# A window of four on the swapped weight loads of a recurrent attention kernel

## The chip, the cores and the metric

The kernel runs on one core of one Trainium2 chip. A core has a matrix engine (PE, with its weight loads shown apart as PEld), a vector engine (DVE), a scalar engine (ACT), a general engine (POOL) and an engine that only issues DMAs and waits (SP). Sixteen DMA engines move data between the chip's memory (HBM) and the core's on-chip memory. The metric is device time in microseconds (us) of one launch: before the change three runs gave a median of 1762.69 us (1759.73 to 1764.29).

## The reference, cut to what matters

Two branches are computed from `A_x`, 2048 rows of 640, and mixed by a gate. Branch b is a gated feed-forward layer without recurrence. Branch a is an attention over 64 segments of 32 rows: each segment attends over its rows and 8 memory rows, and the first 8 output rows of a segment are the memory of the next one.

```python
mem = mem0                                     # 8 rows of 640
for s in range(64):
    h = concat([mem, x[32*s:32*s+32]])         # 40 x 640
    q, k, v = (einsum('td,dhe->hte', h, W) for W in (Wq, Wk, Wv))   # 32 heads of 192
    p = softmax(where(mask, q @ k.T * scale, -1e9))
    o = einsum('hte,hed->td', p @ v, Wo)       # 40 x 640
    mem = o[:8]
    outs.append(o[8:])
a = concat(outs)
b = (gelu(x @ w_gate) * (x @ w_up)) @ w_down
out = g * a + (1 - g) * b                      # g = sigmoid((x * gate_w).sum(-1))
```

The segments can't be computed at the same time: the memory rows make a chain. Each of the four attention weights has 640 x 6144 numbers of two bytes, 31 MB in all, and each segment uses all of them. The on-chip memory holds most of them but not all.

## The kernel before, in words

**Two stages.** First the feed-forward branch runs for all rows (`ffn_*`, in the trace up to about 195 us); its result goes to a scratch tensor in HBM. Then come the 64 segments, `segment(s)`, of some 24 us each.

**Weights in pieces.** `Wq`, `Wk` and `Wv` are cut into pieces `(m, octet, k)`: matrix 0, 1 or 2, one of four groups of eight heads, and one of five slices of the 640 inputs. Such a piece is 128 partitions of 3072 bytes, 384 KB. `Wo` is cut into 16 pieces `(3, p)` of 128 partitions of 3840 bytes, 480 KB. Nearly all pieces have a place of their own in the big on-chip tensor `arena` and stay there. Sixteen places are shared by two pieces each (`partner`, lines 545 to 552): 13 of the first three matrices (five of V, five of K, three of Q), between octet 0 and octet 3, and three of `Wo`, between the first three and the last three pairs.

**Swapping.** Even segments go through the octets upwards, odd ones downwards (`octet`, line 527). So what a segment uses last, the next one uses first. A segment begins with the pieces that are there; after their last use in this segment `swap_loads` (line 612) loads the partner into the same place, and the partner is used at the segment's end. This makes 16 swapped loads in each of the segments, issued by `load_piece` (line 597; the DMA is line 599). Each place has its own semaphore (`slot0`, `slot1`, ...), which counts 16 when a load has landed; the PE instruction that first uses the piece waits for it.

**Order.** `PROG` (line 506) is an order written out by hand: projections `("g", group, k)`, transposes, scores, softmax, and output projections `("wo", ...)`, among which other work is placed. `_Sched.add` (line 73) records each operation in this order and derives what it has to wait for from the regions that it reads and writes; `finalize` turns these into semaphore waits and leaves out a wait that an earlier one on the same engine has covered (`wm`, `snap`). Each engine then runs its own list in order. In the segments SP issues all DMAs but two, so SP's list holds, in the order of `PROG`: the swapped loads of K and Q, the loads of V, the store of the last segment's output (`out_store`, line 956), the load of the next segment's rows (`x_load`, line 706), the last V piece, stores of prepared rows for later segments (`left_evac`, line 1276, and `left_store`, line 895), three `Wo` pieces, and loads of prepared rows and of branch b (`stg_load`, line 935; `bz_load`, line 947; `bzl_load`, line 952). A swapped load waits for the PE work that read the old piece. SP does nothing else while it waits, and what stands behind in its list isn't issued.

**The lines of PE** that are named below: 1046 and 226 are the projections, 884 those of prepared rows, 1087 to 1100 the scores, 1144 and 1149 the transposes of the softmax, 1177 and 1179 the products with v, 1206 and 1229 the output projection. Line 1375 is the DVE transpose that hands the memory rows to the next segment.

Of the kernel before, what the change touches and what calls it, by code (L numbers as in the profile page):

```python
# [231 lines left out]
def _build(nc, A_x, A_mem0, A_Wq, A_Wk, A_Wv, A_Wo, seg_len, w_gate, w_up, w_down,  # L232
# [34 lines left out]
    S_ = _Sched(nc)  # L267
# [82 lines left out]
    def bview(o, nbytes, plo=0, phi=128):  # L350
        return arena[plo:phi, o // 2:(o + nbytes) // 2]
# [4 lines left out]
    def sreg(o, nbytes, plo=0, phi=128):  # L356
        return Rg("sb", o, o + nbytes, plo, phi)
# [133 lines left out]
    def piece_src(key):  # L491
        if key[0] == 3:
            return Wo2[:, key[1]]
        m, o_, k = key
        return (Wq2, Wk2, Wv2)[m][:, k, OW * o_:OW * (o_ + 1)]

    def piece_size(key):
        return GO if key[0] == 3 else GQ

    def piece_view(key, o):  # L500
        if key[0] == 3:
            return bview(o, GO).rearrange("p (c n) -> p c n", n=Dm)
        return bview(o, GQ)
# [59 lines left out]
    res_off = {}  # L563
# [8 lines left out]
    r_res = {key: sreg(o, piece_size(key)) for key, o in res_off.items()}  # L572
# [13 lines left out]
    slot_id = {}  # L586
# [6 lines left out]
    later = []  # L593

    loaded = {}

    def load_piece(key, name):
        loaded[slot_id[key]] = key
        S_.add("sp", lambda e: e.dma_start(piece_view(key, res_off[key]), piece_src(key)), writes=[r_res[key]],
               dma_sem="slot%d" % slot_id[key], name="%s %s" % (name, key))  # L600

    def piece(seg, key):
        order = orders[seg % 2]
# [8 lines left out]
    def swap_loads(seg, item):  # L612
        if item[0] == "g" and item[1] == 0 and 0 < item[2] < KT - 1:
            later.extend(key for key in done_keys if key[0] == 1)
            done_keys[:] = [key for key in done_keys if key[0] != 1]
        elif later:
            done_keys[:] = sorted(done_keys + later, key=lambda key: key[:1] + key[2:])
            del later[:]
        for key in done_keys:
            other = swap_in.get(key)  # L620
            if other is None or (other in partner) == (seg % 2 == 0):
                continue
            load_piece(other, "swap s%d" % seg)
        del done_keys[:]
# [11 lines left out]
    def load_residents(cls, pick=lambda key: True):  # L636
        for key in first:
            if slot_class[key] == cls and pick(key):
                load_piece(partner[key] if key in tmp_off else key, "res")
# [39 lines left out]
    for h in range(NH):  # L679
        for w_, sb_, rw_, nm in ((w_gate, wg_sb, r_wg, "wg"), (w_up, wu_sb, r_wu, "wu")):  # L680
            S_.add("sp", lambda e, h=h, w_=w_, sb_=sb_: e.dma_start(
                sb_[h], w_.rearrange("(p k) f -> p k f", p=128)[:, :, FH * h:FH * (h + 1)]),
                writes=[rw_[h]], dma_sem="%s%d" % (nm, h))
# [228 lines left out]
    for n, (g, o) in enumerate(units):  # L912
# [7 lines left out]
        if g == 0:  # L920
            S_.add("pool", lambda e, o=o, b=b: e.tensor_copy(out=stg[o // 2][:, o % 2], in_=lst[b][:, 0]), reads=[r_lst[b]], writes=[r_stgh[o // 2][o % 2]],
                   name="stg s0 o%d" % o)
# [498 lines left out]
def bass_gated_mix__memory_aug_recurrent_mem_tr__glu_gated_geglu__prompt_kernel(  # L1421
    nc,
    A_x,
    A_mem0,
    A_Wq,
    A_Wk,
    A_Wv,
    A_Wo,
    A_seg_len,
    B_x,  # L1430
    B_w_gate,
    B_w_up,
    B_w_down,
    gate_w,
    out,
):
    _build(nc, A_x, A_mem0, A_Wq, A_Wk, A_Wv, A_Wo, A_seg_len, B_w_gate, B_w_up, B_w_down, gate_w, out)
# [33 lines left out]
```

## Time and profile before

| what | value |
|---|---|
| median of three runs | 1762.69 us (1759.73 to 1764.29) |
| span of the profiled execution, which is also its own time | 1765.1 us |
| PE busy | 1623.9 us, 92% |
| DVE, ACT, POOL busy | 960.0, 802.8, 320.0 us |
| granted PE clock, mean | 0.994 |
| moved by DMA | 499.57 MB, mean 283 GB/s |
| time of the DMA engines taken by SP's and ACT's DMAs (q1 and q10) | 78.3% and 0.6% |
| chain that ended last, by engine | PE 71%, DVE 15%, DMA 6%, issue 4%, ACT 4% |
| median from issue to landing, pieces of Wq, Wk, Wv, Wo | 5.4, 7.1, 9.1, 6.4 us |

The profile shows one execution. A group of instructions is named by its line, engine, output and inputs; "idle before" is the time the engine waited before these instructions, with what ended the wait. "Issue" there means that no semaphore explains the wait. SP's instructions are only the issues of DMAs; when a transfer has landed is told by the last update of its semaphore. The trace also holds a record of each DMA packet with its queue, start, duration and size, and of all semaphore updates. The span's first 195 us are the feed-forward stage; 1550 of the 1765 us are segments.

### The profile page before, as it was taken

Reading aid. Unit: us, or ns where it says so; the run is one execution under the profiler, and the core shown is the slowest. Engines: PE = TensorE matmul, PEld = TensorE weight load, DVE = VectorE, ACT = ScalarE, POOL = GpSimd, SP = SyncE. Lnnn points to the kernel's source line nnn. Section 1 sums busy time; section 2 is a strip of 40 time slices with the busy share of each in tenths; the row PEclk is TensorE's granted clock in tenths of the full one; section 3 lists DMA queues with packets and bytes.
Section 4 is the critical chain, followed back from the end, with each engine's and each line's share of the span. In section 5 each row is a group of like instructions: output and inputs, shape, how many; then the busy total and the mean of one; then the engine's idle time right before and its main releaser. Section 6 shows DMA issues by size and latency. Waiting matters only on the chain.

```text
span 1765.1 us, 80301 instructions
## 1 busy us (share of the span) xinstructions
PE 1623.9 (92%) x39162; PEld 809.5 (46%) x31501; DVE 960.0 (54%) x2932; ACT 802.8 (45%) x1835; POOL 320.0 (18%) x1099
## 2 busy tenths in 40 slices
PE   9999999999999999999999989999999998999887
PEld 4554444444444444454444444454444444454444
DVE  2222655556555655555555655555555655655554
ACT  3222544545444544444444544444444544445443
POOL 1100111111112112111212111111211121121211
PEclk9999999999999999999999999999999999999999
DMA  9814987888778887888788887879787886879776
GB/s 335 295 48 157 329 313 250 320 313 288 280 269 311 299 308 253 315 290 319 281 280 293 296 293 250 314 285 323 279 280 275 311 310 241 312 282 327 283 275 238
DMA packets 271311, 499.57 MB, mean 283 GB/s; under 512 B 105304, under 2 KB 132208, under 8 KB 270960
## 3 DMA queue, kind: packets, MB, share of 16 engines
q1 hardware_dynamic: 267832, 491.34, 78.3%
q8 instruction: 276, 4.52, 1.0%
q10 hardware_dynamic: 3128, 3.09, 0.6%
q14 instruction: 75, 0.61, 0.1%
HBM read 473.22 MB, written 21.11 MB: 280 GB/s over the span
## 4 chain that ended last, share of the span: by engine, by line
PE 71%; DVE 15%; DMA 6%; issue 4%; ACT 4%; DVEq 0%; SPq 0%; ACTq 0%
PE ps L1046 20%; PE ps L226 15%; PE ps L1206 8%; DMA arena<-in_A_Wo_dram 5%; PE ps L1177 3%; PE ps L804 3%; PE ps L801 3%; PE ps L884 3%; PE ps L1100 3%; PE ps L819 2%; PE ps L1087 2%; DVE ps L1114 2%; DVE arena L1112 2%; PE ps L1095 2%; PE ps L1229 2%
## 5 line engine op out<-in xcount | busy, mean ns | idle before, releaser
L1046 PE MATMUL ps<-arena 128*32 128x384 bf16 x9940 | 723.0, 329 | 42.4 <-DVE arena L1375 34.4
L226 PE MATMUL ps<-arena 128*32 128x384 bf16 x7680 | 595.4, 328 | 7.9 <-DVE arena L1215 3.5
L1046 PEld LDWEIGHTS ps<-arena 128*32 128x32 bf16 x9940 | 257.5, 97 | 365.3 <-issue 226.0
L1080 DVE STREAM_TRANSPOSE arena<-arena 128x384 bf16<-128x384 bf16 x512 | 270.8, 557 | 150.8 <-ACT arena L1066 149.2
L1066 ACT ACTIVATE arena<-ps 128x384 bf16<-128x384 f32 x512 | 236.2, 489 | 211.6 <-PE ps L1046 196.3
L1206 PE MATMUL ps<-arena 128*32 128x320 bf16 x6144 | 293.6, 301 | 13.9 <-issue 13.4
L1124 ACT ACTIVATE ps<-ps 104x160 f32<-104x160 f32 x256 | 71.9, 281 | 293.4 <-DVE ps L1114 293.4
L1206 PEld LDWEIGHTS ps<-arena 128*32 128x32 bf16 x6144 | 163.5, 97 | 74.0 <-issue 19.4
L1112 DVE TENSOR_REDUCE arena<-ps 104x4 f32<-104x160 f32 x256 | 83.0, 324 | 165.8 <-PE ps L1100 164.6
L941 POOL COPY arena<-arena 128x96 bf16<-128x96 bf16 x256 | 70.3, 275 | 513.4 <-PE ps L1100 444.2
L1188 ACT ACTIVATE arena<-ps 128x480 bf16<-128x480 f32 (+1 forms) x256 | 137.0, 535 | 43.8 <-PE ps L1179 39.6
L1196 POOL COPY arena<-arena 128x96 bf16<-128x96 bf16 x256 | 68.3, 267 | 441.1 <-ACT arena L1188 357.3
L1162 ACT ACTIVATE arena<-ps 128x448 bf16<-128x448 f32 x192 | 104.2, 543 | 96.7 <-PE ps L1149 96.4
L1069 ACT ACTIVATE arena<-ps 128x384 bf16<-128x384 f32 x256 | 125.1, 489 | 20.9 <-PE ps L1046 16.3
L1177 PE MATMUL ps<-arena 128*64 128x160 bf16 x1536 | 123.1, 243 | 12.5 <-ACT arena L1162 6.9
L1126 DVE TENSOR_REDUCE arena<-ps 104x4 f32<-104x160 f32 x256 | 83.0, 324 | 92.5 <-ACT ps L1124 92.5
L1177 PEld LDWEIGHTS ps<-arena 128*64 128x64 bf16 x1536 | 80.8, 109 | 91.6 <-issue 31.7
L884 PE MATMUL ps<-arena 128*32 128x384 bf16 x1280 | 111.4, 330 | 2.2 <-issue 2.0
L1179 PE MATMUL ps<-arena 128*64 128x64 bf16 x1536 | 104.8, 193 | 4.1 <-issue 4.1
L891 DVE STREAM_TRANSPOSE arena<-arena 128x384 bf16<-128x384 bf16 x128 | 73.7, 576 | 31.6 <-ACT arena L889 27.8
L1215 DVE TENSOR_TENSOR arena<-ps,arena 64x160 f32<-64x160 f32 x160 | 50.8, 317 | 72.3 <-ACT arena L1212 61.6
L1114 DVE TENSOR_TENSOR ps<-ps,arena 104x160 f32<-104x160 f32 x256 | 85.0, 332 | 8.8
(84 smaller groups left out, 1819.2 us busy)
## 6 DMA issues: line engine op xcount, KB each, us to landing
arena<-in_A_Wk_dram SPq DMA_DIRECT2D x335, 384.0 KB, 7.1
arena<-in_A_Wv_dram SPq DMA_DIRECT2D x335, 384.0 KB, 9.1
arena<-in_A_Wo_dram SPq DMA_DIRECT2D x205, 480.0 KB, 6.4
arena<-in_A_Wq_dram SPq DMA_DIRECT2D x209, 384.0 KB, 5.4
arena<-left_qk_scratch SPq DMA_DIRECT2D x126, 96.0 KB, 2.8
left_qk_scratch<-arena SPq DMA_DIRECT2D x49, 192.0 KB, 2.3
left_qk_scratch<-arena SPq DMA_DIRECT2D x30, 96.0 KB, 5.7
ffn_b_scratch<-arena ACTq DMA_DIRECT2D x16, 160.0 KB, 4.4
```

The costliest lines, as they stand in the source:

```text
L226: return e.add_instruction(mybir.InstMatmult(name=nm, start_tensor_calc=like["start"], stop_tensor_calc=stop, tile_size=(128, 32), tile_po ...
L884: fns.append(lambda e, outp=outp, rhs=rhs, j=j: e.matmul(outp, lhs, rhs, start=(k == 0), stop=(k == KT - 1), tile_position=(0, 32 * j)))
L1046: fns.append(lambda e, outp=outp, rhs=rhs, j=j: e.matmul(outp, lhs, rhs, start=(k == 0), stop=(k == KT - 1), tile_position=(0, 32 * j)))
L1066: S_.add("act", lambda e, m=m, bk=bk: e.activation(out=rows_sb[m], in_=ps[:, bk, 0:384], func=ACTF.Copy), reads=[r_ps[bk]], writes=[r_rows ...
L1069: S_.add("act", lambda e, i=i, bk=bk: e.activation(out=v_sb[i % NVB].rearrange("p (c n) -> p c n", c=3), in_=ps[:, bk, 0:384].rearrange("p ...
L1080: S_.add("dve", lambda e: e.transpose(out=dst[:, :, 0:L], in_=rows_sb[m].rearrange("p (c r) -> p c r", r=L)), reads=[r_rows[m]], writes=[r ...
L1112: S_.add("dve", lambda e: e.tensor_reduce(out=mxs, in_=S3, axis=AX.X, op=ALU.max), reads=[rb], writes=[rst], name="smax max")
L1114: S_.add("dve", lambda e: e.tensor_tensor(out=S3, in0=S3, in1=mxb, op=ALU.subtract), reads=[rb, rst], writes=[rb], name="smax sub")
L1177: return [lambda e: e.matmul(full, v[:, e0:e0 + 64], PTm[:, i], start=True, stop=False, tile_position=(0, 64 * i), skip_group_check=True), ...
L1179: lambda e: e.matmul(part, vl[:, e0:e0 + 64], PTl[:, i], start=False, stop=True, tile_position=(0, 64 * i), skip_group_check=True)]
L1188: S_.add("act", lambda e: e.activation(out=apx(u[:, 0, 0, :], [[R, na], [3 * R, 4], [1, R]]), in_=ps[:, A, 0:na * W].rearrange("p (c t r) ...
L1206: fns.append(lambda e, i=i, t=t, j=j, gv=gv: e.matmul(ps[32 * j:32 * j + 32, bank, 0:2 * DJ].rearrange("p (h n) -> p h n", h=2), lhs2[i], ...
```

## The change

At most four swapped loads are under way. `load_piece` keeps a list of the swapped loads that were issued last; each further one gets, beside the waits that it had, a wait for the landing of the fourth last one. Loads whose name doesn't begin with "swap" (the first filling of the places) are not counted and get no wait. No operation is added to PE, ACT, DVE or POOL, and the order on every engine is the one of before.

```diff
     loaded = {}
+    NUW = 4
+    under_way = []
 
     def load_piece(key, name):
         loaded[slot_id[key]] = key
-        S_.add("sp", lambda e: e.dma_start(piece_view(key, res_off[key]), piece_src(key)), writes=[r_res[key]],
-               dma_sem="slot%d" % slot_id[key], name="%s %s" % (name, key))
+        op = S_.add("sp", lambda e: e.dma_start(piece_view(key, res_off[key]), piece_src(key)), writes=[r_res[key]],
+                    dma_sem="slot%d" % slot_id[key], name="%s %s" % (name, key))
+        if name.startswith("swap"):
+            under_way.append(op)
+            if len(under_way) > NUW:
+                op.deps.add(under_way.pop(0))
```

In the built program SP's list has 764 loads that wait for a landing of a place, where it had 7: twelve in each segment, since the first four of a segment wait for loads whose landing SP already knows from a wait on PE. Most of these loads also wait for PE; an instruction carries one wait, so 504 separate wait instructions are added to SP's 1795 instructions. The waits of PE are the same.

## The prediction

> **What bounds the kernel now.** I read the page first, then the waits of PE, the chain in one window, SP's own timeline, the DMA table, and last the packet records.
>
> ```profile
> span 1765.1 us, 80301 instructions
> PE 1623.9 (92%) x39162; PEld 809.5 (46%) x31501; DVE 960.0 (54%) x2932; ACT 802.8 (45%) x1835; POOL 320.0 (18%) x1099
> q1 hardware_dynamic: 267832, 491.34, 78.3%
> q8 instruction: 276, 4.52, 1.0%
> ```
>
> PE is the bound, with some 141 us idle. The last line matters here: a second queue brings instructions, 276 packets of 4.52 MB / 276 = 16,384 bytes. PE and PEld have 70,663 instructions, 256.0 per packet, so these packets are PE's instructions, 64 bytes each, one packet per 256.
>
> ```profile
> PE ps L1046 <- DVE arena L1375: 34.4, 48, 1.2
> PE ps L1144 <- DVE arena L1131: 25.0, 65, 0.7
> PE ps L1206 <- issue: 13.4, 14, 2.0
> ...
> PE ps L1229 <- DMA arena<-in_A_Wo_dram: 6.1, 10, 2.3
> ...
> PE ps L1046 <- issue: 5.4, 8, 1.3
> PE ps L1177 <- issue: 4.8, 6, 1.5
> PE ps L1179 <- issue: 4.1, 6, 1.3
> ```
>
> These are PE's waits (total us, times, longest). It waits for swapped weights only 6.6 us (6.1 and 0.5 for one Wk row), so the loads are nearly hidden. It waits 34 us in 48 gaps for nothing that a semaphore explains. Each of these 48 gaps ends 2.2 to 2.7 us after the start of a 16,384-byte packet: PE stood without instructions. The chain of waits between 564 and 569 us shows the third longest, whose packet started at 565.23:
>
> ```profile
> 565.32 0.51 PE ps L1206 x9
> 565.83 1.76 issue
> 567.59 0.72 PE ps L1206 x15
> ```
>
> Now SP in one segment (start, us, engine, line, operation, tiles, count):
>
> ```profile
> 600.65 2.17 SPq L599 DMA_DIRECT2D arena<-in_A_Wq_dram  x3
> 602.86 2.24 SPq L599 DMA_DIRECT2D arena<-in_A_Wk_dram  x4
> 605.15 2.58 SPq L599 DMA_DIRECT2D arena<-in_A_Wv_dram  x4
> 607.77 0.57 SPq L956 DMA_DIRECT2D out_dram<-arena  x1
> 608.38 0.47 SPq L706 DMA_DIRECT2D arena<-x_scratch  x1
> 608.90 0.43 SPq L599 DMA_DIRECT2D arena<-in_A_Wv_dram  x1
> ```
>
> An issue takes about 0.48 us, so twelve swaps are given out in 8 us, but they land 0.97 us apart (a DMA engine takes 0.121 us for a packet of 3072 bytes, and each has 8 of a piece). So up to nine are outstanding, and the DMA table shows it as time from issue to landing:
>
> ```profile
> arena<-in_A_Wk_dram SPq DMA_DIRECT2D x335, 384.0 KB, 7.1
> arena<-in_A_Wv_dram SPq DMA_DIRECT2D x335, 384.0 KB, 9.1
> ```
>
> **The added wait, on the loads.** Twelve loads of a segment are issued later. In the segment above, the last V load was issued at 608.90; it would now wait for the V load that landed at 614.39. It landed at 618.47, as its turn came. So the question is whether the engines ever run out of work. Four pieces are 4 x 0.97 = 3.88 us. The round trip is the time from a landing to the landing of a piece issued then on an empty queue. The first swap of a segment is the nearest row: its first packet starts 0.96 to 1.2 us after the issue's start, and it lands 3.3 us (least, queue empty) to 3.8 us (median of 63, other small transfers ahead) after. SP needs 0.1 us to go on after a wait (median 0.08 from release to the end of an issue that was waiting), 0.4 more where a separate wait instruction comes first. So the round trip is 3.4 to 3.9 us, under or at the 3.88. It is a cold start besides; in a running queue the slowest engine still has two pieces before it when the new one arrives. Carried through all segments in SP's order, a round trip of 3.6 us makes none of the 16 loads later by more than 0.12 us in the mean. I take 0; for the upper bound I take 4.2 us, between the median first swap and the slow ones (4.6 us): 0.3 us lost per round, three rounds, 0.9 us at a segment's end. Less than 0 is excluded as long as PE releases the places when it did: no load is issued earlier, and the order is kept.
>
> **What is queued behind on SP.** `out_store`, `x_load`, stores of prepared rows (L1276), `stg_load`, `bz_load` are issued 1 to 5 us later. They use the same queue behind the same loads: the `x_load` of 608.38 landed at 617.46, between two V loads. Waiting for them are POOL's copies, POOL is 18% busy, and they land when they did. The last swaps, of Wo, are issued about 1 us later, and after them SP is free again: 6 us idle in the segment shown. I take 0. The 504 more instructions on SP cost at most 504 x 0.06 us over 1550 us, beside the waiting.
>
> **The added wait, on instruction fetches.** The same DMA engines serve both queues. From the packet records and PE's instruction count I took for each fetch how far PE had got beyond the earliest point at which neighbouring fetches start. With no swap outstanding that is 0.95 us (median), with one to three 1.6 to 1.8, with four 2.8, with five to nine 3.0 to 3.7. So a fetch stands behind what has already been given to its engine, up to some 3.3 us. By the time to the last landing: over 4 us to go, 179 fetches with 46 stalls of 33.0 us; under 4 us, 83 fetches with one of 0.5 us.
>
> With the window the last landing is never more than about 3.9 us off (4.8 with Wo pieces of 1.2 us), and the newest piece reaches the engines only after 0.6 to 1.0 us, so 1.7 to 2.7 us of work stand before a fetch, where 3.3 or so stood. That cuts a fetch by 0.6 to 1.6 us. Cutting every gap by 0.5 us would take 20.5 of the 34 us, by 1.0 us 29.3. I take nearly all. Bounds: 0 (the row for four outstanding, little below the rows above it) and 34.
>
> **What is late next.** PE comes earlier, the loads don't. From each landing to the first PE instruction that waits for it, the smallest value of a segment is under 0.1 us in 21 of 64 segments and 1.5 us in the median. Where a gap goes, I count per segment only as much as this smallest value: 21.8 of the 34 us. It is cautious, since a stall ahead of the piece's release also moves the load.
>
> **Sum.** 1765.1 - 21.8 + 0 = 1743 us for the profiled execution, which lies 2.4 us above the median of the three runs; against the median I say **1742**, 1.2% faster. Its own range is 1729 (all 34 us) to 1757.
>
> **A rule against it.** The fetch's delay grows with the swaps outstanding, 0.95 to over 3 us, as above. The Trainium skill, DMA: Bandwidth & Descriptors, section Queues, rings and completion order, says that each DMA engine goes round the queues that have work, packet by packet; by that a fetch would wait no longer for nine pieces than for four, and the time would stay 1763. The trace speaks against it in the delays, at least for the first four pieces. The Trainium skill, Runtime: NRT & Kernel Launch, section Instruction fetch mechanics, calls the crossing of a block "mostly hidden"; by that there is nothing to gain either. 48 gaps of 34 us say that here it isn't wholly.
>
> **Rivals.** (A) No difference. An engine may take in a fixed amount, and four pieces may be enough to fill it: the delay flattens at five, and four are already at 2.8 of 3.3 us. Then gaps shrink by 0.3 us at most and what is won goes into waits for Wo: 1763, between 1758 and 1768. Against it: four outstanding in the rows of before are four wholly handed over; in the window the fourth is mostly still on its way.
>
> (B) Slower: the queue runs dry. Place: from the fifth swap of each segment. It decides from a round trip over 3.88 us. At 4.2 us the last loads are 0.9 us late; 21 segments have no room for that. Counted per segment as above, lateness of 0.2, 0.5 and 1.0 us gives -15.6, -4.6 and +18.7 us with the gaps gone, and +27 us with the gaps kept; it turns at 0.6 us. So 1.0 us gives 1781. For it: 5% of the issues take over 1.1 us instead of 0.43, and the median first swap takes 3.8. Against it: those are cold starts.
>
> **How the numbers follow.** The forecast has 0.62, A 0.18, B 0.20. The bound between a difference and none is 0.3%, 5.3 us, about what runs can tell (three runs spread over 4.6 us). The forecast is all faster, A the same, B slower. Range: the forecast's lower end with a little left out, 1732, up over A and into B as far as half its chance, 1771; some 0.1 is left out above, 0.05 below.
>
> **What would show it.** SP: waits in L601 on landings of Wk, Wq and Wv, hundreds of them; issue to landing of Wk and Wv falls from 7.1 and 9.1 to about 4. PE: "issue" falls from 34 to under 10 us. PE's waits for in_A_Wo_dram rise from 6.1 us, to 10 or 20. DMA bytes unchanged, and landings within a segment still 0.97 us apart: if they are 1.05 or more, B is right. If "issue" stays near 34 us, A is. The prediction would be wrong if a fetch is delayed by something that goes along with outstanding swaps but isn't caused by them, such as the DMA engines' rate itself, which stays.

## The result, and the profile after

The kernel became slower. The changed kernel takes 1834.15 us (median of four runs, 1829.96 to 1844.28); the kernel before took 1761.21 us beside it (four runs, 1754.96 to 1764.29). The ratio is 1.043, with an interval of 1.039 to 1.047. The forecast was 1742 us.

The profiled execution took 1829.96 us, with a span of 1828.2 us, 63.1 us more than the span of before. The lines behind the change stand six lower than before (the load itself is L601 instead of L599), so L1046, L1206 and L1229 are now L1052, L1212 and L1235. From the page of the changed kernel, its span, PE's busy time, the two DMA queues and the chain that ended last by engine:

```profile
span 1828.2 us, 80824 instructions
PE 1647.4 (90%) x39181; PEld 800.3 (44%) x31501; DVE 964.1 (53%) x2932; ACT 803.0 (44%) x1835; POOL 321.0 (18%) x1099
q1 hardware_dynamic: 267832, 491.34, 80.4%
q8 instruction: 276, 4.52, 1.0%
PE 59%; DMA 25%; DVE 11%; ACT 3%; issue 2%; SPq 0%; DVEq 0%; ACTq 0%
```

The packets and the bytes are those of before. In the chain, DMA went from 6% to 25% and "issue" (of any engine there) from 4% to 2%: the loads, which had hardly counted, now hold a quarter of it. PE's busy time also grew, by 23.5 us, though it does the same work. The waits of PE (total us, times, longest) say the same:

```profile
PE ps L1235 <- DMA arena<-in_A_Wo_dram: 52.0, 64, 3.0
PE ps L1052 <- DVE arena L1381: 31.3, 48, 0.7
PE ps L1150 <- DVE arena L1137: 27.9, 70, 0.7
PE ps L1052 <- DMA arena<-in_A_Wv_dram: 21.6, 31, 1.7
...
PE ps L1212 <- issue: 2.4, 3, 0.9
...
PE ps L1235 <- issue: 0.8, 2, 0.6
```

All "issue" waits together fell from 33.9 us in 48 gaps to 3.9 us in 7. All waits for DMA rose from 6.8 to 75.8 us: for `Wo` from 6.1 to 52.0, for V from nearly nothing to 21.6. The waits for DVE are where they were. So the 63.1 us are 23.5 of PE's busy time, 69.0 of waits for loads, 30.0 saved of "issue", and 0.6 of everything else.

The table of DMA issues (KB each, median us from issue to landing) answers the one of before:

```profile
arena<-in_A_Wk_dram SPq DMA_DIRECT2D x335, 384.0 KB, 4.9
arena<-in_A_Wv_dram SPq DMA_DIRECT2D x335, 384.0 KB, 4.7
```

They were 7.1 and 9.1 us. With four under way, 4.9 us from issue to landing means one landing each 4.9 / 4 = 1.225 us. Without the window the mean of a segment's first twelve landings had been one each 1.109 us. One segment on SP's timeline (start, us, engine, line, operation, tiles, count) shows how it goes:

```profile
646.49 1.72 SPq L601 DMA_DIRECT2D arena<-in_A_Wq_dram  x3
649.29 3.64 SPq L601 DMA_DIRECT2D arena<-in_A_Wk_dram  x4
653.61 3.52 SPq L601 DMA_DIRECT2D arena<-in_A_Wv_dram  x4
657.18 0.59 SPq L962 DMA_DIRECT2D out_dram<-arena  x1
657.82 0.46 SPq L712 DMA_DIRECT2D arena<-x_scratch  x1
659.23 0.33 SPq L601 DMA_DIRECT2D arena<-in_A_Wv_dram  x1
660.16 2.47 SPq L601 DMA_DIRECT2D arena<-in_A_Wo_dram  x3
```

Four K pieces that went out in 2.2 us now take 3.6, and the last V piece goes out 12.7 us after the first Q piece, where it was 8.3. Inside this run, a K piece issued at 650.25 us, right behind a Q landing at 650.23, landed at 654.51, 4.26 us later; the V piece issued at 653.61 landed at 659.16, 5.55 us later. Both are above the 3.88 us that the forecast took four pieces to last. SP's own waits show what held it:

```profile
SPq L601 <- DMA arena<-in_A_Wk_dram: 192.8, 197, 3.1
SPq L601 <- DMA arena<-in_A_Wq_dram: 139.0, 154, 2.7
```

Over 62 segments, the means of the landings relative to the segment's first swap issue are, in us (worked out from the semaphore updates; pieces 14 to 16 are those of `Wo`):

```
piece    1     4     8     12     16
before  3.93  7.70 12.04  16.13  21.35
after   3.73  7.47 12.43  17.21  23.47
```

For four pieces there is no loss, as nothing waits. From the fifth on it grows, to 2.1 us at the end of the segment. About half of that shows in the time of a segment, which rose from 24.65 to 25.65 us.

### The profile page after: what moved, and what is told of

It reads as the page before. It is cut to its first block, busy times and chain, and to the rows that moved or that the text cites. A ratio compares the mean times of both kernels' runs of the same rounds, so it can differ in the third digit from the quotient of the medians.

```text
span 1828.2 us, 80824 instructions
## 1 busy us (share of the span) xinstructions
PE 1647.4 (90%) x39181; PEld 800.3 (44%) x31501; DVE 964.1 (53%) x2932; ACT 803.0 (44%) x1835; POOL 321.0 (18%) x1099
## 4 chain that ended last, share of the span: by engine, by line
PE 59%; DMA 25%; DVE 11%; ACT 3%; issue 2%; SPq 0%; DVEq 0%; ACTq 0%
DMA arena<-in_A_Wo_dram 18%; PE ps L1052 17%; PE ps L226 14%; PE ps L1212 5%; DMA arena<-in_A_Wv_dram 3%; PE ps L810 3%; PE ps L807 3%; DMA arena<-in_A_Wk_dram 3%; PE ps L1106 2%; PE ps L825 2%; PE ps L1183 2%; PE ps L1093 2%; DVE ps L1120 2%; PE ps L890 2%; PE ps L1101 2%
## 5 line engine op out<-in xcount | busy, mean ns | idle before, releaser
L1052 PE MATMUL ps<-arena 128*32 128x384 bf16 x9940 | 734.9, 334 | 56.0 <-DVE arena L1381 31.3
L226 PE MATMUL ps<-arena 128*32 128x384 bf16 x7680 | 607.3, 335 | 8.9 <-DVE arena L1221 3.5
L1052 PEld LDWEIGHTS ps<-arena 128*32 128x32 bf16 x9940 | 259.4, 98 | 400.7 <-issue 227.1
L1086 DVE STREAM_TRANSPOSE arena<-arena 128x384 bf16<-128x384 bf16 x512 | 270.9, 558 | 157.3 <-ACT arena L1072 155.8
L1212 PE MATMUL ps<-arena 128*32 128x320 bf16 x6144 | 283.4, 299 | 2.4 <-issue 2.4
L1212 PEld LDWEIGHTS ps<-arena 128*32 128x32 bf16 x6144 | 158.1, 96 | 57.9 <-issue 3.7
L1235 PE MATMUL ps<-arena 128*32 128x160 bf16 x3072 | 82.2, 235 | 58.6 <-DMA arena<-in_A_Wo_dram 52.0
L890 PE MATMUL ps<-arena 128*32 128x384 bf16 x1280 | 108.2, 330 | 0.0
L1235 PEld LDWEIGHTS ps<-arena 128*32 128x32 bf16 x3072 | 53.3, 96 | 108.5 <-DMA arena<-in_A_Wo_dram 68.7
```

What stands on the lines that cost most here:

```text
L226: return e.add_instruction(mybir.InstMatmult(name=nm, start_tensor_calc=like["start"], stop_tensor_calc=stop, tile_size=(128, 32), tile_po ...
L890: fns.append(lambda e, outp=outp, rhs=rhs, j=j: e.matmul(outp, lhs, rhs, start=(k == 0), stop=(k == KT - 1), tile_position=(0, 32 * j)))
L1052: fns.append(lambda e, outp=outp, rhs=rhs, j=j: e.matmul(outp, lhs, rhs, start=(k == 0), stop=(k == KT - 1), tile_position=(0, 32 * j)))
L1086: S_.add("dve", lambda e: e.transpose(out=dst[:, :, 0:L], in_=rows_sb[m].rearrange("p (c r) -> p c r", r=L)), reads=[r_rows[m]], writes=[r ...
L1212: fns.append(lambda e, i=i, t=t, j=j, gv=gv: e.matmul(ps[32 * j:32 * j + 32, bank, 0:2 * DJ].rearrange("p (h n) -> p h n", h=2), lhs2[i], ...
L1235: S_.add("pe", [lambda e, j=j, c=c, g_=g_, p=p: e.matmul(ps[32 * j:32 * j + 32, OB2, SC:512], u[:, p % 4, c, 0:L], g_[:, c, DJ * j:DJ * (j ...
```

## The experiments

Three readings of this were to be told apart. **T**: the queue runs dry. The round trip of a piece in a running queue is about 4.9 us and four pieces don't fill it; with more pieces outstanding the loss goes. **S**: the loss comes from SP being held in the waits, with the other DMAs in its list behind it. **W**: the loss comes from the 504 added wait instructions themselves, whatever the number they wait for. A fourth, **V**, was added for the halves of pieces below: what counts is only the number of bytes under way, not the number or size of the pieces.

### The size of the window

The edit changes one number, to 3, 5, 6 or 8:

```diff
-    NUW = 4
+    NUW = 6
```

> Window of three instead of four. Theory T (the DMA engines run dry): with four, the trace of the changed kernel shows 4.85 us from issue to landing in the middle of a segment, 3.05 us until the first of the 16 engines has finished its share and 1.75 us more until the last has; that is 1.21 us per swap against 1.11 us before. With three the round trip stays at 4.6 to 4.85 us, 1.55 us per swap: thirteen swaps 0.44 us later each, 5.7 us at a segment's end, of which some 1.1 us is covered: 1760 + 62 x 4.6 = about 2045 us (1980 to 2110). Rival S (what stands behind the waiting SP is late, whatever the engines do): SP is held back by the landing of the third instead of the fourth last, 1.2 us more: 1834 + 62 x 1.2 = about 1910. Rival W (the 504 further wait instructions cost the time): as with four, 1834.

> Window of five. T: 5 x 1.11 = 5.5 us of work against a round trip of 4.85, the engines hardly run dry: landings 1.11 to 1.13 us apart as before, 1750 to 1775 us, PE's unexplained waits (issue) between the 4 us with four and the 34 us without a window. S: SP is still held in each segment from the sixth load on, about 1.1 us less than with four: 1834 - 25 = about 1810. W: 1834.

> Window of six. T: no engine runs dry for the window's sake: 1745 to 1765 us; if fetches are still shortened, issue on PE below 25 us and the time below 1755. S: SP is held less, half of the loss stays: about 1790. W: 1834.

> Window of eight, reached only late in a segment (before, up to nine were outstanding). T: as before the change, 1755 to 1765 us, issue on PE about 30 us. S: 1760 to 1775. W (the further wait instructions are all still there): 1834.

Measured, with the changed kernel (window 4) and the one before (no window) among them. Issue to landing is that of a piece behind a full window (in the row "none", of a piece with about eight others under way), split into the time to the first of the 16 engines' updates and the spread from there to the last; the waits of PE and the stretches at half clock (from the trace's clock records) are those of the profiled execution, in us:

```
window median   ratio (95%)               issue to landing    /N    DMA    issue half clock
3      1994.31  1.131 (1.126 to 1.136)    2.78 + 1.45 = 4.23  1.41  187.7   0    204.8
4      1834.15  1.043 (1.039 to 1.047)    3.20 + 1.70 = 4.90  1.23   75.8   3.9   67.4
5      1789.43  1.013 (1.008 to 1.017)    3.77 + 1.96 = 5.73  1.15   32.2  23.2   48.2
6      1760.72  0.9987 (0.9959 to 1.0015) 4.59 + 2.15 = 6.74  1.12   13.9  27.7   10.7
8      1769.81  1.0028 (1.0005 to 1.0052) 6.35 + 2.19 = 8.54  1.07    6.9  38.5    6.4
none   1762.54                            7.25 + 2.04 = 9.29   -      6.8  33.9   23.6
```

T's number for a window of three, 1980 to 2110 us, was met; S's 1910 and W's 1834 were not. It was met near its lower end, and T's reason only in part: T let the round trip stay at 4.6 to 4.85 us, and it fell to 4.23. In a window of three DMA has 38% of the chain that ended last. The page has a span and a busy time of PE of

```profile
span 1985.0 us, 80887 instructions
PE 1703.3 (86%) x39181; PEld 816.5 (41%) x31501; DVE 965.3 (49%) x2932; ACT 804.2 (41%) x1835; POOL 321.2 (16%) x1099
```

and PE waits for V and `Wo`, with no "issue" line left among its waits:

```profile
PE ps L1052 <- DMA arena<-in_A_Wv_dram: 104.7, 90, 3.4
PE ps L1235 <- DMA arena<-in_A_Wo_dram: 76.5, 78, 3.5
```

W is out by all four: windows of six and eight have wait instructions of the same kind, and stand at 0.9987 and 1.0028. The instructions are thus worth at most the 9 us of the latter interval's end. S expected 1790 us for a window of six and is out there, too: SP stands 323 us in waits for landings of swapped loads in that run (541 us with the window of four), and it costs nothing. For a window of five T expected 1750 to 1775 and S about 1810, and 1789 was measured, which is neither: the round trip of a fuller queue is longer still (5.73 us against 5 x 1.11 = 5.55 us of work), so five pieces are just short. For a window of eight T expected 1755 to 1765; 1769.8 is a little above, and within S's 1760 to 1775, so that run speaks for neither. In the window of five both kinds of waits of PE stand side by side:

```profile
PE ps L1235 <- DMA arena<-in_A_Wo_dram: 27.9, 34, 2.7
...
PE ps L1235 <- issue: 10.6, 13, 1.7
```

At six the first is nearly gone and the second is back:

```profile
PE ps L1235 <- DMA arena<-in_A_Wo_dram: 12.4, 17, 2.1
PE ps L1052 <- issue: 8.2, 14, 1.1
```

and at eight it is nearly all "issue":

```profile
PE ps L1212 <- issue: 12.3, 13, 1.6
PE ps L1052 <- issue: 9.3, 12, 1.2
```

So the two effects cross, and at no size tried did the loss through loads and the gain on fetches leave anything: the window of six, the best, can't be told from the kernel before. The column "/N", issue to landing over the window, is the time per landing when the window is full. It falls from 1.41 to about 1.07 to 1.12 us, which is the rate without a window; from there more pieces only wait longer at the engines. No version was faster than the kernel before by more than its interval.

### Halves by partitions

To keep the bytes of four pieces under way but wait in smaller steps, each swapped load was cut into two DMAs of 64 partitions, each with its own semaphore; the window then counts halves: eight (`half8`, the bytes of four pieces), ten, twelve, and none (`half_free`, the control).

```diff
-    NUW = 4
+    NUW = 8
...
+        for h in range(2):
+            op = S_.add("sp", lambda e, h=h: e.dma_start(piece_view(key, res_off[key])[64 * h:64 * h + 64], piece_src(key)[64 * h:64 * h + 64]),
+                        writes=[sreg(res_off[key], piece_size(key), 64 * h, 64 * h + 64)],
+                        dma_sem="slot%d%s" % (slot_id[key], "b" * h), name="%s %s" % (name, key))
```

> Each swapped piece is loaded by two DMAs, partitions 0 to 63 and 64 to 127, each with its own semaphore; at most eight such halves are under way, so as many bytes as with a window of four pieces, but counted in finer steps. Theory T (the engines run dry because a whole round trip, 3.05 us to the first engine's end and 1.75 us of spread between the engines, stands against the work in the window): a half has four packets less per engine, 4 x 0.121 = 0.48 us, so the round trip is 4.85 - 0.48 = 4.4 us against 8 x 0.555 = 4.4 us of work: the engines are just kept busy, 1765 to 1800 us. Rival V (the bytes in flight, or SP being held by landings, set the rate, whatever the step): as with four pieces, 1815 to 1850 us. Against both: 32 issues of 0.48 us are 15.4 us of a segment's 24.6 on SP; the run without a window tells what that costs.

> The same halves with no window: the control. Both theories: 1755 to 1775 us, PE's unexplained waits (issue) about 34 us as before. If SP's doubled issues cost something it shows here.

> Ten halves under way, the bytes of five pieces (which gave 1789 us). T: 10 x 0.555 = 5.55 us of work against 4.4 to 4.6 us: 1750 to 1768 us, issue on PE 15 to 25 us. V: 1780 to 1795 us.

> Twelve halves, the bytes of six pieces (1761 us). T: 1752 to 1765 us, issue on PE about 28 us. V: 1755 to 1768 us. Tells whether halves as such cost anything where the window doesn't.

The forecasts of all four runs, the control's too, lie between 1750 and 1850 us and were missed. All four take the same time: half8 2297.82 us (ratio 1.302, 1.295 to 1.308), half_free 2299.05 (1.304, 1.297 to 1.311), half10 2294.67 (1.299, 1.291 to 1.306), half12 2295.82 (1.299, 1.292 to 1.306). The cut itself costs 30%, with or without a window. From the page of the control, its DMA packets and one line of its issues:

```profile
DMA packets 287575, 499.70 MB, mean 217 GB/s; under 512 B 121560, under 2 KB 148464, under 8 KB 287216
```

```profile
arena<-in_A_Wv_dram SPq DMA_DIRECT2D x640, 192.0 KB, 6.5
```

The bytes are the same but they move at 217 GB/s instead of 283. In the packet records a packet of 3072 bytes takes 0.20 us (median) where it took 0.121, one of 3840 bytes 0.258 where it took 0.149, and an issue on SP, with the pause behind it, takes 0.64 us where it took 0.48. Why the packets are slower isn't shown. The loads have become the bound: a piece is 8 x 0.20 = 1.6 us of work for each engine, and PE waits 340 us for DMA. A half takes 6.23 us from issue to landing behind a full window of eight, and eight halves are 8 x 4 packets x 0.20 = 6.4 us of work, so this window covers its round trip; it hardly binds (SP waits 71 us for landings of swapped loads, against 541 us in the changed kernel) and costs nothing over its control (-1.2 us). These runs were meant to tell T from V and don't; they give the price of the cut, and one thing on the fetches, below.

### Halves by columns

The same with each piece cut along the row of every partition, so that a half still spans 128 partitions, with packets of 1536 bytes:

```diff
+    def half(x, h):
+        n = x.shape[1] // 2
+        return x[:, h * n:(h + 1) * n]
...
+        for h in range(2):
+            op = S_.add("sp", lambda e, h=h: e.dma_start(*(half(x, h) for x in (bview(res_off[key], piece_size(key)), piece_row(key)))),
+                        writes=[sreg(res_off[key] + h * (piece_size(key) // 2), piece_size(key) // 2)],
+                        dma_sem="slot%d%s" % (slot_id[key], "b" * h), name="%s %s" % (name, key))
```

> Control for finer steps: each swapped piece is loaded by two DMAs, each of all 128 partitions and half of the columns, so that packets are 1536 instead of 3072 bytes and all engines and partitions take part (the halves by partitions ran at 0.20 us per packet of 3072 bytes instead of 0.121, and hid the window). No window. A packet should take about 0.065 us (768 bytes take 0.036, 3072 take 0.121), a piece 1.04 us instead of 0.97: 1765 to 1800 us.

> Eight column halves under way, the bytes of four pieces, in finer steps. Theory T (the engines run dry in a round trip of 4.85 us, of which 1.75 are the spread between first and last engine): a half shortens the round trip by its missing 8 x 0.055 = 0.45 us to 4.4 us; eight halves are 8 x 0.58 = 4.6 us of work: 0 to 25 us over col_free. Rival V (bytes in flight, or SP being held by landings, set the rate whatever the step): 60 to 80 us over col_free, as four pieces are over no window.

> Ten column halves, the bytes of five pieces. T: 5.8 us of work against 4.4 to 4.6: -15 to +5 us against col_free, with PE's unexplained waits (issue) at 15 to 25 us instead of 34. V: 20 to 35 us over col_free, as five pieces were 27 us over no window.

> Twelve column halves, the bytes of six pieces. Both: within 10 us of col_free; T with issue on PE about 25 to 30 us.

Measured, with the waits of PE in us:

```
                  median   ratio (95%)             DMA   issue  half clock
col_free          1846.28  1.045 (1.042 to 1.048)  69.2  1.2     76.5
col8              1909.18  1.081 (1.077 to 1.086)  99.5  0.8    107.9
col10             1859.20  1.052 (1.049 to 1.056)  82.4  0.5     80.2
col12             1856.60  1.051 (1.048 to 1.054)  74.6  2.5     77.8
```

Here the control costs 4.5%, where 1765 to 1800 us were forecast. Two things in its records make its loads slower. A packet of 1536 bytes takes 72.1 ns on average, so a piece takes each engine 16 x 0.0721 = 1.154 us instead of 8 x 0.1324 = 1.059. And SP needs 0.51 us for an issue and 0.06 between two, 1.14 us for a piece, so it is no faster than the engines and has mostly seven halves outstanding when it issues the next, eleven at most. Against this control a window of eight halves costs another 63 us, one of ten 13 and one of twelve 10. The 63 are what V forecast (60 to 80, T 0 to 25); the 13 are neither V's 20 to 35 nor T's -15 to 5, and the 25 to 30 us of "issue" that T expected with twelve are 2.5. The window of eight costs its 63 us although SP waits only 82 us for landings of swapped loads in it, a quarter of its waits in the window of six pieces, which costs nothing. That is the second point against S. The lines of PE's waits in col_free (L1248 and L1065 are here what L1235 and L1052 are in the changed kernel),

```profile
PE ps L1248 <- DMA arena<-in_A_Wo_dram: 43.9, 107, 1.5
```

and in col8,

```profile
PE ps L1248 <- DMA arena<-in_A_Wo_dram: 62.0, 144, 1.6
...
PE ps L1065 <- DMA arena<-in_A_Wv_dram: 27.7, 59, 1.3
```

show the same places as in the changed kernel. And the table of issues of col8 has the same time to landing as that for whole pieces,

```profile
arena<-in_A_Wv_dram SPq DMA_DIRECT2D x640, 192.0 KB, 4.4
```

behind a full window 2.89 us to the first engine and 1.94 of spread, 4.83 us in all. Half the size of a step did not shorten it. That part of T, by which smaller steps at the same bytes should have come round sooner, fell, and V fits: four pieces of 393,216 bytes over 4.90 us are 321 GB/s, eight halves over 4.83 us are 326 GB/s. So four pieces' worth of bytes have a round trip of some 4.85 us in either cut. The support is weaker than it was meant to be, since SP's own pace keeps the control close to that number of bytes, too.

Col_free also bears on the fetches. It has no window and yet only 1.2 us of "issue", with mostly seven halves outstanding, the bytes of three and a half pieces. That is what the reading of the "issue" gaps asks for: they go with the bytes outstanding. But another thing can make them go. In `half_free` PE has only 2.4 us of "issue", too, and there the fetches are as late as before the change. Counted from the earliest point of PE's list at which the six fetches on either side start, the delay is over 3 us in 80 of 260 fetches before, in 21 of 260 after, in 30 of 260 in `col_free` and in 78 of 262 in `half_free`. In `half_free` PE waits 340 us for loads and a fetch starts only each 7.9 us (median) instead of 5.9. That fits a PE that is too slow there to run out of instructions, so few "issue" gaps alone don't show that fetches are short.

## Why the prediction was wrong

**Instruction fetches: right in direction and size.** The text took the 34 us of "issue" as PE standing without instructions while a fetch stood behind loads, and expected less than 10 us to stay. 3.9 us stayed. A fetch's delay at four swaps outstanding was 2.8 us in the rows of before; under the window of four it is 2.04 us (median of 175 fetches), a cut of 1.3 us from the 3.3 or so of a full queue, inside the 0.6 to 1.6 us of the text. That also settles rival A, by which 2.8 us were to stay: as the text held against it, four in a window are not yet four that stand before the engines. In the windows of five, six and eight it is 2.68, 3.00 and 3.2 to 3.7 us, and the stalls come back with it: 23.2, 27.7 and 38.5 us. The objection that the text raised against itself, that the delay may go along with outstanding swaps without being caused by them, is not borne out: the bytes were the same and the mean rate little different (273 against 283 GB/s), only the number outstanding was set. That shorter fetches alone took the stalls away is not shown, since PE now also waits 69.0 us longer for loads; PE's median time between two fetches (5.8 us against 5.9) says that its pace changed little. By the Trainium skill (DMA: Bandwidth & Descriptors, section Queues, rings and completion order) an engine goes round its queues packet by packet, so the depth of one queue should not matter to the other; over the range that the windows set, the trace disagrees.

**"The added wait, on the loads", lateness taken as 0: this step failed.** It set a round trip of 3.4 to 3.9 us against 4 x 0.97 = 3.88 us of work. The measured round trip is 4.90 us, above the 4.2 that it took as the upper bound, and the lateness at a segment's last landing is 2.1 us where 0 to 0.9 were allowed. Two terms were off.

- The round trip was taken from the first swap of a segment. It lands 3.93 us after its issue, of which 2.83 are to the first engine's update and 1.10 the spread over the sixteen. Behind a full window they are 3.20 and 1.70. The text named the missing part, that "in a running queue the slowest engine still has two pieces before it when the new one arrives", and priced it at nothing beyond 4.2 us.
- The 0.97 us per landing came from one undisturbed stretch of one segment. The mean over the first twelve landings of all segments of before is 1.109. It is nearer the rate that can be held, and it did not help: at 1.109, a window of four would have needed a round trip of 4.4 us.

The Trainium skill (DMA: Bandwidth & Descriptors, section Latency and other measured facts) gives HBM access as 0.2 us on average and 2 us under high load, and calls it the main part of a DMA's fixed cost. The runs agree in kind: issue to landing is longer in a busy queue than at a segment's start. How much of the 1.0 us between them is the memory's, no run here tells.

**Rival B, "the queue runs dry": right in place, direction and test, wrong in size.** It named the fifth swap as the place, and that is where the landings part. Its turning point was 0.6 us of lateness and its price 1781 us for 1.0. At 2.0 us the text's own count per segment, continued, gives +72.5 us with the stalls gone; the span grew by 63.1. The two numbers are not quite the same thing, since the count knows nothing of the clock, below. The text's test between the two was the distance of landings: "if they are 1.05 or more, B is right". They are 1.225. As a test it was worth little, because the mean before the change was 1.109 already; what speaks for B is the step from 1.109 to 1.225.

**What was not in the sum at all: PE's clock.** The trace's clock records show stretches at half clock, of 3.4 us or multiples of it: six with 23.6 us before, 16 with 67.4 after. Half of the 43.8 us that were added is 21.9, and PE's busy time grew by 23.5. The other windows agree: in that of three, half of the added time is 90.6 us and PE's busy time grew by 79.4; in that of five, 12.3 and 11.7. (With column halves something else is added: in `col_free` 26.5 and 54.5.) The mean matmul of L1052 (L1046 before) went from 329 to 334 ns, that of L226 from 328 to 335. The middle of the span shows it with the granted clock in the third column from the end. First before, then after (window, its length, busy us and count of PE, PEld, DVE, ACT and POOL, granted clock, DMA share, GB/s):

```profile
615.00:1015.00 400.00, 369.05 (x9718) 184.89 (x7770) 232.69 (x725) 192.13 (x448) 76.98 (x268) 1.00 0.82 293
```

```profile
615.00:1015.00 400.00, 361.23 (x9284) 173.61 (x7376) 222.84 (x692) 183.76 (x429) 74.79 (x259) 0.97 0.84 280
```

The Trainium skill (TensorE: Matmul & The Clock Gate, section What's actually happening) has the clock halved after an idle window of about 3.4 us and given back after a busy one. The length of the stretches agrees. That the window has to be idle does not: no wait of PE on its list of after is longer than 3.0 us. The trace shows what comes before a stretch. All 16 begin on one grid of steps of 3.413 us, and in the step ahead of each, PE was busy for 14% to 57% of the time. Of the other 498 steps at full clock, PE was busy for no more than 57% in 13. So several short waits that together leave PE about half idle for one step are enough here. How much of the time the clock alone costs was not separated by a run of its own: it rises and falls with the waits for loads (204.8 us in the window of three, 10.7 in that of six), and a wait for a load is both.

**What the engines did.** In the two rows above the DMA engines are busy for a larger share (0.84 against 0.82) and move less (280 against 293 GB/s). Engines that merely stood empty would not show that. Between the fourth and the twelfth landing of the segments, the time of the packets was 1.03 of the engines' time before and 0.95 after (packets overlap a little), and the rate fell from 390 to 318 GB/s; the mean packet of 3072 bytes took 124 ns before and 143 after. Over all segments the median packet stays at 121 ns, but those over 200 ns went from 3695 to 7294. So "the queue runs dry" is only a part of it: the larger part of the lost rate is packets that take longer when few pieces are under way. In the window of six both are back (1.03, 125 ns, 387 GB/s). What makes the packets longer is not shown.

**"What is late next" and PE's waits.** (The sum, 1762.7 - 21.8, is 1741 and not 1742, which changes nothing.) The text expected waits for `Wo` of 10 or 20 us; they are 52.0, and 21.6 for V come on top, as follows from the lateness. Of Wk and Wv it expected "about 4" us to landing, and 4.9 and 4.7 were measured; that one number, over the window's four pieces, is most of the mistake.

**What is queued behind on SP, taken as 0: right as far as the runs go.** In the window of six SP is held for 323 us and the kernel loses nothing, and the chain of after has no more of SP in it than that of before (SPq 0%).

**Open.** Whether part of the lateness could be regained by waiting on a part of a landing instead of the whole was not tried. What causes the spread between the sixteen engines is not shown, nor why more packets are slow behind a short queue. No run takes the shorter fetches without the later loads, so what they are worth alone is open.

## What to carry to other kernels

Here a limit on the loads under way was a limit on the rate: so many bytes over the time from issue to landing in a running queue. That time has to be read where the queue is full and to the last engine's update, not from the first load after a pause (here 4.9 against 3.9 us, which is 4.3% of the kernel), and the pieces have to cover it with one or two to spare (here six of 384 KB). And where a matrix engine waits for nothing that a semaphore explains, it is worth laying the instruction fetches beside the outstanding loads: here it was a real cost, but one that shorter queues only exchanged for late data.

## What was not expected of the hardware

- Two DMAs of 64 partitions in place of one of 128 move the same packets of 3072 bytes at 0.20 us each instead of 0.121, an issue on SP, with the pause behind it, takes 0.64 us instead of 0.48, and the kernel's rate falls from 283 to 217 GB/s.
- Between the first and the last of the sixteen engines' updates of one load lie 1.1 us after a pause and 1.7 to 2.2 us with four or more loads under way, more than one piece's time at an engine.
- PE's clock was halved for stretches of 3.4 us or multiples though no wait of PE was longer than 3.0 us: 16 times here, each after a step of 3.413 us in which PE was busy for 57% or less. In the window of three, where the longest wait is 3.5 us, it was 41 times, 204.8 us in all, each after a step with 54% or less.
- Late instruction fetches did not show as waits of PE where PE was held up otherwise: 78 fetches that were over 3 us late went with 2.4 us of "issue" in `half_free`, and 80 with 33.9 before the change.
